# A fused attention and two-MLP kernel: another step table for the attention work inside the first MLP, and another placing of nine weight conversions

## The chip, the cores and the metric

One Trainium2 chip, one core. The metric is the device time of one execution in microseconds (us), the median of three runs. Engines are named as the profile names them: PE (TensorE matmul) and PEld (its weight loads), DVE (VectorE), ACT (ScalarE), POOL (GpSimd), SP (the engine that issues most transfers).

## What is computed

Inputs are float32. Attention has 4 batches, 8 heads, 576 rows of 64, each row looking at itself and the 63 before it. Its output is the input of a first MLP with a layer norm ahead of it, and that one's output is the input of a second block that mixes the tokens and then the channels.

```python
scores = scale * np.matmul(q, k.transpose(0, 1, 3, 2))
mask = (rel >= 0) & (rel < 64)
attn = softmax(np.where(mask, scores, -1e9))
x = (attn @ v)                                # 4 x 576 x 512
xn = (x - mu) / np.sqrt(var + 1e-06) * g_ln
x = x + np.maximum(xn @ w_ch1, 0.0) @ w_ch2   # first MLP, 512 -> 2048 -> 512
h = np.maximum(xt @ w_tok1, 0.0) @ w_tok2     # second block, over the tokens
u = x + h.transpose(0, 2, 1)
out = u + np.maximum(u @ w_ch1, 0.0) @ w_ch2  # 512 -> 1536 -> 512
```

## The kernel before

The 2304 rows are 18 tiles of 128. The first MLP runs in five blocks of tiles, `BLOCKS`: 3, 3, 4, 4 and 4 tiles; they are called blocks 0 to 4 here. Every product is made from float32 numbers split in a high and a low part, in three passes, so a product of a 128-row chunk takes three matmuls.

**A block** is `mlp_block` (L430): 16 steps f, one for each 128 columns of the hidden layer. In a step `mm1` (L400) makes the hidden chunk `ha` with 12 matmuls (L409), ACT takes its positive part (L413) and DVE the low part of that (L421, called the low part below); then `mm2` (L424) adds an earlier chunk, `LAG` = 2 steps back, into the accumulators `acca` (L427, three matmuls for each tile of the block). Between the two stand the step's hooks, functions that issue other work. `ha` has two buffers in PSUM (tag `h`), so the matmuls of `ha` of step f+2 need the low part of step f done. In block 1 the `mm2` of two steps stand together, after the odd steps. At the end of a block ACT and DVE write the next block's normalized input (L373, L374) and DVE adds the accumulators to the rows (L879).

**The hooks of blocks 1 to 3** make the attention of the next block's four tiles, by the table `STEPS` (L752): one string per step, for block 1 and for blocks 2 and 3. In it

- S is the scores of a tile: 32 small matmuls (L207), 8 maxima with the mask on DVE (L220) and 8 exponentials on ACT (L228), and then the loads of the next tile's q and k; `S4` belongs to the next block's first tile
- T*n is n of the 16 transposes of 32x256 on DVE that turn a tile's probabilities (L275)
- V is their product with v (32 matmuls into `o`, L312), the division by the sums on DVE (L318) and the load of the next v. From tile 10 on (blocks 2 and 3) `o` is one of the two buffers of `ha`
- L is the row statistics and the centring on ACT (L336 to L338), with two small POOL operations
- X*n is n of the 16 transposes of the centred rows of two tiles on DVE (L390)

A digit after S, T, V, L is the tile in its block of four, after X the pair. What stands in a step's string is issued in that order behind the step's low part, and each engine runs its instructions in the order of issue.

**The pieces.** Nine blocks of later weights come in 64 bits per number and are turned into a high and a low float32 part, in the same blocks. The table `EARLY` (L732) gives a place in `xs` and steps g = 16 (block - 1) + f: at g - 2 SP issues the load (L622), at g ACT shrinks (L130) and DVE narrows (L139, L140), at g + 1 ACT and POOL split (L122, L123), at g + 2 SP issues the store to DRAM (L641). `piece_raw`, `piece_narrow` and `piece_split` (L616 to L636) name the buffers: two rows of `xs` and a third for the narrowed words.

**Block 4** has no attention: its hooks convert the second block's first weights (b_narrow L720, w1_mix L677, w1_plain L685, w1_mixed L692, w1_keep L697), two per two steps, with scratch from the list `narrows` (L101).

**The second block** ends in `quad` (L1000), seven products per call into two PSUM buffers; ACT copies the first one to the scratch `s1` (L1013), which the last low part of the call before still reads.

```python
 752          STEPS = ((),
 753                   ("V0 S1 L0", "T1*6", "T1*8", "T1*2", "V1 S2 L1", "T2*6", "T2*8", "T2*2 X0*6", "V2 S3 L2", "X0*5 T3*3",
 754                    "T3*8", "T3*5 X0*5", "V3 L3 S4", "X1*8", "X1*8"),
 755                   ("T0*10", "T0*6", "V0 S1 L0", "T1*6", "T1*10", "V1 S2 L1", "T2*6", "T2*6", "T2*4 X0*4", "V2 S3 L2",
 756                    "X0*6 T3*3", "T3*8", "T3*5 X0*6", "V3 L3 S4", "X1*6", "X1*10"))
```

Of the kernel before, what the change touches and what calls it, by code (L numbers as in the profile page):

```python
# [12 lines left out]
U32 = mybir.dt.uint32  # L13
# [5 lines left out]
B, H, S, D = 4, 8, 576, 64  # L19
# [5 lines left out]
T1 = 256  # L25
# [49 lines left out]
def mixer_kernel(ctx, tc, qT, kT, v, g, wa1, wa2, tok1, tok2, wb1, wb2, out):  # L75
# [44 lines left out]
    def split(dst_hi, dst_lo, src, lo_engine):  # L120

        nc.scalar.activation(out=dst_hi, in_=src, func=AF.Copy)  # L122
        lo_engine.tensor_tensor(out=dst_lo, in0=src, in1=dst_hi.bitcast(F32), op=ALU.subtract)  # L123
# [134 lines left out]

    whole, wholeT, sums = {}, {}, {}

    def tile_S(t):

        whole[t] = by_heads(wide_a)
        sums[t] = stp.tile([P, 2, NH, 1], F32, tag="sums", name=f"sums{t}")
        att_S(t, False)
        for u in (2 * t, 2 * t + 1):
            att_E(u)

    def tile_T_part(t, n):
# [58 lines left out]
    def ln_scalar(t):  # L328

        m_ = mv[t] = mvp.tile([P, 2], F32, tag="mv", name=f"mv{t}")  # L330
        if t < BLOCKS[2][0]:
            x_, y_ = xh[t], _ = next_s(), next_s()
        else:
            j = (t - BLOCKS[2][0]) % 4
            x_, y_ = (lns[:, 2], lns[:, 3], reg[:, 1], reg[:, 9])[j], reg[:, 8]
        nc.scalar.activation(out=x_, in_=xt[t], func=AF.Copy, scale=-1.0 / DM, accum_out=m_[:, 0:1])  # L336
        nc.scalar.activation(out=x_, in_=xt[t], func=AF.Identity, bias=m_[:, 0:1])
        nc.scalar.activation(out=y_, in_=x_, func=AF.Square, accum_out=m_[:, 1:2])  # L338
        nc.gpsimd.tensor_scalar(out=m_[:, 1:2], in0=m_[:, 1:2], scalar1=1.0 / DM, scalar2=LN_EPS,  # L339
                                op0=ALU.mult, op1=ALU.add)  # L340
        nc.gpsimd.tensor_tensor(out=m_[:, 1:2], in0=m_[:, 1:2], in1=mhalf, op=ALU.pow)
# [109 lines left out]
    with tc.manual_schedule():  # L451
# [162 lines left out]
        early = {}  # L614

        def piece_raw(x):  # L616
            return xs[:, x:x + 2].rearrange("p t n -> p (t n)")

        def piece_load(x, piece):
            early[x] = piece  # L620
# [8 lines left out]

        def piece_narrow(x):  # L630
            n = piece_width(x)
            narrow([(xs[:, x + 2, 0:n].bitcast(U32), piece_raw(x)[:, 0:2 * n].bitcast(U32))])

        def piece_split(x):
            n, pair = piece_width(x), piece_raw(x).rearrange("p (a n) -> p a n", a=2).bitcast(F32R)
            split(pair[:, 0, 0:n], pair[:, 1, 0:n], xs[:, x + 2, 0:n], nc.gpsimd)  # L636

        def piece_keep(x):
            pair = piece_raw(x).rearrange("p (a n) -> p a n", a=2)
# [89 lines left out]

        EARLY = {12: (12, 17, 21), 15: (14, 18, 22, 26, 30, 34)}  # L732
        pieces = [t1_piece(0), t1_piece(1), t2_piece(0), t2_piece(1), rest_piece()]
        pieces += [w2_piece(q, k) for q in range(2) for k in range(2)]
        starts = sorted((g_, x) for x, gs in EARLY.items() for g_ in gs)
# [6 lines left out]
        def early_hooks(g_, hooks):  # L742
            for d, fn, x, piece in sorted(at[g_], key=lambda e: -e[0]):
# [4 lines left out]
                else:  # L748
# [1 line left out]


        STEPS = ((),  # L752
# [4 lines left out]
        done = collections.Counter()  # L757


        for i in range(NBLOCKS):  # L760
            hooks = {f: [] for f in range(FA + 2)}
            if i < NBLOCKS - 1:
                u0 = 2 * TPB * (i + 1)
                lean = i == 0

                def next_qk(t):
                    if t + 1 < NT:
                        place_fixed(t + 1)
                        load_qk(t + 1)

                def next_v(t):
                    if t + 1 < NT:
                        load_v(t + 1)

                for k in range(2 * TPB if lean else 0):
                    def s1(u=u0 + k):
                        new_x(u // 2)
                        att_S(u // 2, True)
                        next_qk(u // 2)

                    def s3(u=u0 + k):
                        att_PV(u // 2, (u % 2,))
                        if u % 2 == 1:
                            next_v(u // 2)
                            ln_stats(u // 2)

                    u, t = u0 + k, (u0 + k) // 2
                    fs, ft, fv = LEAN[k]
                    if k % 2 == 0:
                        hooks[fs].append(s1)  # L790
                    hooks[ft].insert(0, lambda u=u: att_T(u))
                    hooks[fv].append(s3)
                    if k % 2 == 1:
                        hooks[fv + 1].append(lambda t=t: ln_center(t))

                def step(op, t, n):
                    if op == "S":
                        new_x(t)
                        tile_S(t)
                        next_qk(t)  # L800
                    elif op == "V":
                        tile_PV(t)
                        next_v(t)
                    elif op == "L":
                        ln_scalar(t)
                    else:
                        (tile_T_part if op == "T" else xh_part)(t, n)

                for f, ops in enumerate(STEPS[min(i, 2)]):
                    for op in ops.split():  # L810
                        what, _, n = op.partition("*")
                        a = what[0], int(what[1]) + (0 if what[0] == "X" else BLOCKS[i + 1][0])
                        for _ in range(int(n or 1) if a[1] < NT else 0):
                            hooks[f].append(lambda a=(*a, done[a] % 16): step(*a))
                            done[a] += 1

                if lean:
                    hooks[FA - 2].append(lambda: step("S", 2 * TPB, 0))
                if i == NBLOCKS - 2:
                    hooks[FA - 1].append(lambda: b_load(2))  # L820
                for f in range(FA):
                    early_hooks(FA * (i - 1) + f, hooks[f])

                def tr3(i=i):
                    for c in range(3):
                        trans("a", xh, i + 1, c)
                if lean:
                    hooks[FA - 1].append(tr3)
                    for hh in range(2):
                        hooks[FA + hh].append(lambda hh=hh: tile_T_PE(2 * TPB, hh))  # L830

                def after(i=i):
                    if i > 0:
                        u_ = lns.rearrange("p j (c n) -> p c j n", c=KD)
                        for c in range(KD):
                            gained(xn4[:, c], c, u_[:, c], j=4)
                    else:
                        for c in range(3):
                            evac(c)
                        trans("a", xh, i + 1, 3)  # L840
                        evac(3)
            else:
                def ysk(k):
                    new_ys(0, k)
                    for t in range(2 * k, min(2 * k + 2, 9)):
                        y_split(t, nc.gpsimd)
                for f in range(1, 2 * HALF + 1):
                    hooks[f - 0.5] = [b_narrow]
                    hooks[f].append(b_shrink)
                for k, q in enumerate(ORDER):  # L850
                    hooks[2 * k + 2].append(lambda q=q: w1_mix(q))
                    hooks.setdefault(2 * k + 2.5, []).insert(0, lambda q=q, k=k: w1_plain(q, MIX_SLOT[k]))
                    hooks.setdefault(2 * k + 3.5, []).append(lambda q=q: w1_mixed(q))
                    if k < 4:
                        hooks[2 * k + 5].append(lambda q=q: w1_keep(q))
                for f, k in ((11, 0), (12, 1), (13, 2), (14, 3), (15, 4)):
                    hooks[f].append(lambda k=k: ysk(k))
                hooks[13].append(load_t1)
                hooks[14].append(lambda: load_t2(0))
                hooks[15].append(lambda: load_t2(1))  # L860

                def after():
                    pass
            if i == 0:
                later_s += [narrows.pop(), narrows.pop()]
                for f in range(FA):
# [4 lines left out]
                hooks[FA - 2].append(lambda: wnarrow(2))  # L871
            if i == 1:
                narrows[:] = [reg[:, 1]] + [lns[:, k] for k in range(4)]
            base, nt = BLOCKS[i]
            x_, m = places(nt * P), 4 if i == 1 else 3
            acc = mlp_block(i, W, FA, [(xn4 if nt > TPB else xnt)[:, c] for c in range(KD)], hooks, after, i == 1, (x_[0:m], x_[m:2 * m]))
# [120 lines left out]
        def low(role, src):  # L997
            low_h(hx[role], src)

        def quad(n, acc, jobs):  # L1000

# [52 lines left out]
        for p in range(PAIRS):  # L1054
            old = acc
            for q in range(HALF):
# [64 lines left out]
                for m, k, js in ((0, 8, (3, 4)), (0, 9, (5, 0)), (1, 0, (1, 2))):  # L1121
                    if q == m and p > 0:
                        jobs[k] += [lambda j=j, p=p, old=old: store(2 * TPB * (p - 1) + j, old[j]) for j in js]
                quad(n, old if q == 0 else acc, jobs)


        last, half = 2 * TPB * (PAIRS - 1), DM // 2
# [51 lines left out]
```

## Time and profile before

| | us |
|---|---|
| three runs, median | 820.92 (819.51 to 821.58) |
| the profiled execution | 820.49 |
| its span in the trace | 818.7 |
| DVE busy | 500.3 (61%) |
| ACT busy | 324.5 (40%) |
| POOL busy | 175.8 (21%) |

The span is the time from the first to the last recorded instruction; 1.79 us of the profiled execution lie outside it. In the trace block 1 begins at 107.17 us, block 2 at 186.80, block 3 at about 291, block 4 at about 393. A row of the timeline merges instructions of one kind that follow each other: start, length, engine, line, operation, what is written from what, their number, and in brackets the idle time of the engine ahead of it with what ended it. Lengths of merged rows hold the last instruction's latency, so rows can overlap by some tenths. PEclk is the granted clock of TensorE as a share of 2.4 GHz.

### The profile page before, as it was taken

How to read it: one execution, taken by the hardware profiler on the slowest of the kernel's cores; microseconds unless marked ns; L12 is line 12 of the kernel's file. 1: busy time of each engine (PE TensorE's matmuls, PEld its weight loads, DVE VectorE, ACT ScalarE, POOL GpSimd, SP SyncE). 2: the span in 40 equal slices, each digit the busy share in tenths (PEclk: the TensorE clock that was granted, in tenths of full speed). 3: DMA queues.
4: the chain of work that ended last, by engine and by line, in shares of the span. 5: the costliest groups of instructions: out<-in, count | busy, mean ns of one | idle time of the engine just before them, and what ended most of it. 6: DMA issues, size and time to landing. Idle time of an engine off the chain costs nothing.

```text
span 818.7 us, 12590 instructions
## 1 busy us (share of the span) xinstructions
PE 798.7 (98%) x4730; PEld 686.8 (84%) x4730; DVE 500.3 (61%) x1162; ACT 324.5 (40%) x802; POOL 175.8 (21%) x181
## 2 busy tenths in 40 slices
PE   8999989998999989999999999999999999999998
PEld 6788878886888868888888888888988998998997
DVE  5898757788666786566855326756565644742223
ACT  6887643343434324331443422423453222432221
POOL 3655400010110000000033724311134000310000
PEclk9999999998999999999999999999999999999999
DMA  9798321242432222110258315234551624235302
GB/s 338 239 293 280 100 66 52 84 136 79 146 105 86 87 67 79 51 52 27 71 176 317 147 42 208 88 142 152 179 195 79 257 91 175 94 105 219 114 1 77
DMA packets 34284, 108.42 MB, mean 132 GB/s; under 512 B 4912, under 2 KB 6448, under 8 KB 31024
## 3 DMA queue, kind: packets, MB, share of 16 engines
q1 hardware_dynamic: 34080, 107.36, 38.0%
q8 instruction: 37, 0.61, 0.3%
q10 hardware_dynamic: 144, 0.26, 0.1%
q14 instruction: 23, 0.19, 0.1%
HBM read 86.77 MB, written 20.32 MB: 131 GB/s over the span
## 4 chain that ended last, share of the span: by engine, by line
PE 82%; DVE 11%; ACT 5%; issue 1%; POOL 0%; DVEq 0%; ACTq 0%
PE acca L427 19%; PE ha L409 17%; PE accb L984 17%; PE prod L975 16%; DVE reg L275 4%; PE td L911 3%; PE th L897 3%; PE o L312 2%; DVE reg L390 2%; PE s L207 2%; ACT reg L228 2%; DVE hreg L421 1%; PE accb L1135 1%; DVE xnt L374 1%; PE pt L243 1%
## 5 line engine op out<-in xcount | busy, mean ns | idle before, releaser
L409 PE MATMUL ha<-xnt,wa 128*128 128x512 f32 (+1 forms) x960 | 211.2, 370 | 3.1 <-DVE hreg L421 2.3
L427 PE MATMUL acca<-wa,hreg 128*128 128x512 f32 x864 | 211.6, 395 | 0.3 <-DVE hreg L421 0.3
L409 PEld LDWEIGHTS ha<-xnt,wa 128*128 128x128 f32 x960 | 175.2, 188 | 30.2 <-DVE hreg L421 2.6
L427 PEld LDWEIGHTS acca<-wa,hreg 128*128 128x128 f32 x864 | 161.4, 189 | 35.8 <-issue 2.0
L984 PE MATMUL accb<-w,hreg 128*128 128x512 f32 x612 | 142.2, 390 | 0.0
L984 PEld LDWEIGHTS accb<-w,hreg 128*128 128x128 f32 x612 | 114.6, 188 | 23.2
L421 DVE SCALAR_TENSOR_TENSOR hreg<-ha,hreg 128x512 fp32r<-128x512 f32 (+1 forms) x80 | 50.8, 635 | 108.6 <-ACT hreg L413 108.2
L413 ACT ACTIVATE hreg<-ha 128x512 fp32r<-128x512 f32 (+1 forms) x80 | 44.1, 552 | 172.9 <-PE ha L409 167.8
L275 DVE STREAM_TRANSPOSE reg<-reg 32x256 f32<-32x256 f32 x176 | 76.7, 436 | 2.6
L992 POOL TENSOR_TENSOR reg<-reg 128x384 f32<-128x384 f32 x18 | 18.5, 1026 | 211.4 <-ACT reg L989 211.4
L421 DVE SCALAR_TENSOR_TENSOR hreg<-reg,hreg 128x384 fp32r<-128x384 f32 x54 | 33.0, 612 | 45.9 <-ACT hreg L995 45.8
L975 PE MATMUL prod<-xm,w1b 128*128 128x384 f32 x324 | 59.6, 335 | 0.7 <-ACT reg L989 0.6
L989 ACT ACTIVATE reg<-prod 128x384 f32<-128x384 f32 x72 | 35.3, 492 | 62.9 <-PE prod L975 60.3
L228 ACT ACTIVATE reg<-reg,mx 128x128 f32<-128x128 f32 x120 | 46.5, 389 | 29.0 <-DVE mx L220 29.0
L975 PEld LDWEIGHTS prod<-xm,w1b 128*128 128x128 f32 x324 | 56.3, 188 | 1.7 <-ACT reg L989 1.4
L995 ACT ACTIVATE hreg<-reg 128x384 fp32r<-128x384 f32 x54 | 28.1, 525 | 71.7 <-PE accb L984 71.7
L992 DVE TENSOR_TENSOR reg<-prod,reg 128x384 f32<-128x384 f32 x36 | 20.0, 556 | 57.8 <-PE prod L975 56.7
L339 POOL TENSOR_SCALAR mv<-mv 128x1 f32<-128x1 f32 x13 | 2.9, 222 | 222.7 <-ACT reg L338 222.6
L390 DVE STREAM_TRANSPOSE reg<-reg 32x256 f32<-32x256 f32 x96 | 41.7, 434 | 1.5
L975 PE MATMUL prod<-xm,w1a 128*128 128x384 f32 x216 | 41.2, 337 | 0.0
L975 PEld LDWEIGHTS prod<-xm,w1a 128*128 128x128 f32 x216 | 37.8, 188 | 0.6 <-POOL xm L123 0.3
L382 DVE STREAM_TRANSPOSE reg<-xs 32x384 f32<-32x384 f32 x64 | 36.4, 569 | 1.4
(152 smaller groups left out, 953.7 us busy)
## 6 DMA issues: line engine op xcount, KB each, us to landing
xs<-in_wa SPq DMA_DIRECT2D x32, 512.0 KB, 4.8
w1b<-kept SPq DMA_DIRECT2D x16, 1024.0 KB, 7.3
w1a<-kept SPq DMA_DIRECT2D x16, 768.0 KB, 4.7
reg<-in_v SPq DMA_DIRECT2D x28, 256.0 KB, 3.2
reg<-in_wb SPq DMA_DIRECT2D x12, 512.0 KB, 4.1
kept<-w1b SPq DMA_DIRECT2D x6, 1024.0 KB, 7.8
kept<-w1a SPq DMA_DIRECT2D x6, 768.0 KB, 5.7
more<-in_wb SPq DMA_DIRECT2D x8, 512.0 KB, 3.6
```

The source lines that it names most:

```text
L228: nc.scalar.activation(out=f_[:, h], in_=f_[:, h], func=AF.Exp, scale=-1.0, bias=mx[:, h], accum_out=sm[:, h])
L275: nc.vector.transpose(out=s_[32 * b:32 * b + 32, :, 32 * a:32 * a + 32], in_=f_[32 * a:32 * a + 32, :, 32 * b:32 * b + 32])
L382: nc.vector.transpose(out=d_[:, :, :, 32 * a:32 * a + 32], in_=s_[:, :, :, 32 * b:32 * b + 32])
L390: nc.vector.transpose(out=d_[:, :, :, 32 * a:32 * a + 32], in_=s_[:, :, :, 32 * b:32 * b + 32])
L409: nc.tensor.matmul(h_, lhsT=w[:, a, c * P:(c + 1) * P], rhs=src[c][:, b], start=n == 0, stop=n == 3 * KD - 1)
L413: nc.scalar.activation(out=t_[0], in_=h_, func=AF.Relu)
L421: nc.vector.scalar_tensor_tensor(out=t_[1], in0=src, scalar=0.0, in1=t_[0].bitcast(F32), op0=ALU.max, op1=ALU.subtract)
L427: nc.tensor.matmul(acc[j], lhsT=t_[a][:, j * P:(j + 1) * P], rhs=ws[f][:, 2 + b], start=f == first and n == 0, stop=f == last and n == 2)
L975: nc.tensor.matmul(dst, lhsT=w_[:, a, c * P:(c + 1) * P], rhs=xm[m][:, c, b], start=first and n == 0, stop=n == 5, skip_group_check=True)
L984: nc.tensor.matmul(acc[j], lhsT=hx[role][a][:, (j % TPB) * P:(j % TPB + 1) * P], rhs=w2[q][:, k, b], start=q == 0 and role in ("21", "12") ...
L989: nc.scalar.activation(out=dst, in_=src, func=AF.Copy)
L992: eng.tensor_tensor(out=dst, in0=x, in1=y, op=ALU.add)
```

## The change

In blocks 2 and 3, V moves from steps 2, 5, 9, 13 to 3, 6, 10, 13; the first tile's transposes are spread 6, 6, 4 over three steps; L stands one step behind its V; 12 of a tile's 16 transposes stand in the step after its S; X1 ends at step 14. In block 1, V is at 0, 5, 9, 13, the first step's eight exponentials are issued in two halves (H1, E1), and steps 4 and 12 hold no attention. The nine pieces move: two at g = 4, two at 12, then 21, 24, 28, and 53 and 58, in block 4, in other buffers; none is left in block 3. The scratch of L's squares becomes `lns[:, j]`, where it was `reg[:, 8]`, the first half of the T buffer. In block 4 `narrows` has four buffers, not five. The second `quad` call takes another buffer for `s1`.

```diff
-    def tile_S(t):
+    def tile_S(t, half=False):
...
-        for u in (2 * t, 2 * t + 1):
+        for u in (2 * t, 2 * t + 1)[:1 if half else 2]:
             att_E(u)
...
-            x_, y_ = (lns[:, 2], lns[:, 3], reg[:, 1], reg[:, 9])[j], reg[:, 8]
+            x_, y_ = (lns[:, 2], lns[:, 3], reg[:, 1], reg[:, 9])[j], lns[:, j]
...
-            return xs[:, x:x + 2].rearrange("p t n -> p (t n)")
+            return (xs[:, x:x + 2] if x < NT else reg[:, 0:2]).rearrange("p t n -> p (t n)")
+
+        def piece_tmp(x, n):
+            return (xs[:, x + 2] if x < NT else wide_a[:, 1])[:, 0:n]
...
-        EARLY = {12: (12, 17, 21), 15: (14, 18, 22, 26, 30, 34)}
+        EARLY = {12: (4, 12, 21), 15: (4, 12, 24, 28), NT: (53, 58)}
...
-                 ("V0 S1 L0", "T1*6", "T1*8", "T1*2", "V1 S2 L1", "T2*6", "T2*8", "T2*2 X0*6", "V2 S3 L2", "X0*5 T3*3",
-                  "T3*8", "T3*5 X0*5", "V3 L3 S4", "X1*8", "X1*8"),
-                 ("T0*10", "T0*6", "V0 S1 L0", "T1*6", "T1*10", "V1 S2 L1", "T2*6", "T2*6", "T2*4 X0*4", "V2 S3 L2",
-                  "X0*6 T3*3", "T3*8", "T3*5 X0*6", "V3 L3 S4", "X1*6", "X1*10"))
+                 ("V0 H1", "E1", "T1*8", "L0 T1*8", "", "V1 S2", "L1 T2*10", "T2*6", "X0*8", "V2 S3 X0*8", "L2 T3*10",
+                  "T3*6", "", "V3 L3 S4 X1*10", "X1*6"),
+                 ("T0*6", "T0*6", "T0*4", "V0 S1", "L0 T1*12", "T1*4", "V1 S2", "L1 T2*12", "T2*4 X0*6", "X0*10", "V2 S3",
+                  "L2 T3*12", "T3*4", "V3 L3 S4 X1*8", "X1*8"))
...
+            if i == NBLOCKS - 1:
+                del narrows[0]
...
-                quad(n, old if q == 0 else acc, jobs)
+                quad(n, old if q == 0 else acc, jobs, tt[1][:, 0] if n == 1 else s1)
```

ACT at the start of block 1, from the positive part of step 0 (`ha_0`) on; the two rows of L228 are the exponentials of S1's two halves. Before:

```order
L413 ACTIVATE hreg<-ha_0_1386 128x384
L228 ACTIVATE reg,sums_1421<-reg,mx_1440 128x128 x4
L228 ACTIVATE reg,sums_1421<-reg,mx_1445 128x128 x4
L336 ACTIVATE reg,mv_1462<-xs 128x512
L337 ACTIVATE reg<-xs,mv_1462 128x512
L338 ACTIVATE reg,mv_1462<-reg 128x512
L413 ACTIVATE hreg<-ha_1_1468 128x384
```

and with the change:

```order
L413 ACTIVATE hreg<-ha_0_1386 128x384
L228 ACTIVATE reg,sums_1421<-reg,mx_1440 128x128 x4
L413 ACTIVATE hreg<-ha_1_1458 128x384
L228 ACTIVATE reg,sums_1421<-reg,mx_1445 128x128 x4
L413 ACTIVATE hreg<-ha_2_1477 128x384
L413 ACTIVATE hreg<-ha_3_1504 128x384
L336 ACTIVATE reg,mv_1519<-xs 128x512
```

The positive part of step 1 had eight exponentials and L0 ahead of it; four exponentials are left there.

PE at the start of block 2, from `ha` of step 0 to the first V (`o`). Before:

```order
L409 MATMUL ha_0_2150<-xnt,wa_430 128x512 x12
L409 MATMUL ha_1_2177<-xnt,wa_449 128x512 x12
L409 MATMUL ha_2_2203<-xnt,wa_483 128x512 x12
L312 MATMUL o_0_2219<-reg 64x64 x16
L207 MATMUL s_2240<-reg 64x128 x2
```

and with the change:

```order
L409 MATMUL ha_0_2164<-xnt,wa_430 128x512 x12
L409 MATMUL ha_1_2185<-xnt,wa_449 128x512 x12
L409 MATMUL ha_2_2206<-xnt,wa_483 128x512 x12
L427 MATMUL acca_0_2160<-wa_430,hreg 128x512 x3
L427 MATMUL acca_1_2161<-wa_430,hreg 128x512 x3
L427 MATMUL acca_2_2162<-wa_430,hreg 128x512 x3
L427 MATMUL acca_3_2163<-wa_430,hreg 128x512 x3
L409 MATMUL ha_3_2239<-xnt,wa_512 128x512 x12
L312 MATMUL o_0_2254<-reg 64x64 x16
```

The first V stands behind two more groups of 12 matmuls; block 3 begins the same way.

DVE in the same place, from the low part of step 0 to the division of the first V (L318). Before:

```order
L421 SCALAR_TENSOR_TENSOR hreg<-ha_0_2150,hreg 128x512
L275 STREAM_TRANSPOSE reg<-reg 32x8x32 x10
L421 SCALAR_TENSOR_TENSOR hreg<-ha_1_2177,hreg 128x512
L275 STREAM_TRANSPOSE reg<-reg 32x8x32 x6
L252 TENSOR_SCALAR sums_1968<-sums_1968 128x8
L253 RECIPROCAL sums_1968<-sums_1968 128x8
L139 TENSOR_SCALAR xs<-xs 128x512
L140 SCALAR_TENSOR_TENSOR xs<-xs 128x512
L421 SCALAR_TENSOR_TENSOR hreg<-ha_2_2203,hreg 128x512
L318 TENSOR_TENSOR xs<-o_0_2219,sums_1968 128x512
```

and with the change:

```order
L421 SCALAR_TENSOR_TENSOR hreg<-ha_0_2164,hreg 128x512
L275 STREAM_TRANSPOSE reg<-reg 32x8x32 x6
L421 SCALAR_TENSOR_TENSOR hreg<-ha_1_2185,hreg 128x512
L275 STREAM_TRANSPOSE reg<-reg 32x8x32 x6
L421 SCALAR_TENSOR_TENSOR hreg<-ha_2_2206,hreg 128x512
L275 STREAM_TRANSPOSE reg<-reg 32x8x32 x4
L252 TENSOR_SCALAR sums_2004<-sums_2004 128x8
L253 RECIPROCAL sums_2004<-sums_2004 128x8
L421 SCALAR_TENSOR_TENSOR hreg<-ha_3_2239,hreg 128x512
L318 TENSOR_TENSOR xs<-o_0_2254,sums_2004 128x512
```

The 16 transposes stand behind three low parts, where they stood behind two, and the piece (L139, L140) is gone from there.

## Rows read from the trace of the kernel before

**Rows 1.** The page: span, and busy time with its share by engine.

```profile
span 818.7 us, 12590 instructions
PE 798.7 (98%) x4730; PEld 686.8 (84%) x4730; DVE 500.3 (61%) x1162; ACT 324.5 (40%) x802; POOL 175.8 (21%) x181
```

**Rows 2.** Waits of PE, whole span: line, released by, total us, times, longest.

```profile
PE o L312 <- DVE reg L275: 5.6, 5, 2.4
PE o L312 <- DVE hreg L421: 2.9, 2, 1.5
...
PE prod L975 <- ACT reg L989: 0.6, 1, 0.6
...
PE acca L427 <- DVE hreg L421: 0.3, 1, 0.3
```

**Rows 3.** Timeline of PE, step 3 of block 1, idle time in brackets.

```profile
118.35 2.37 PE L409 MATMUL ha<-xnt,wa 128*128 128x384 f32 x12 [2.32 <-DVE hreg L421]
```

**Rows 4.** Timeline of ACT, block 1: first exponential, and positive parts of steps 1, 2.

```profile
112.01 0.40 ACT L228 ACTIVATE reg<-reg,mx 128x128 f32<-128x128 f32 x1 [1.96 <-DVE mx L220]
...
117.24 0.85 ACT L413 ACTIVATE hreg<-ha 128x384 fp32r<-128x384 f32 x2
```

**Rows 5.** Timeline of PE, start of block 2.

```profile
186.80 8.64 PE L409 MATMUL ha<-xnt,wa 128*128 128x512 f32 x36
196.86 0.33 PE L312 MATMUL o<-reg 128*64 128x64 f32 x2 [1.43 <-DVE hreg L421]
199.59 1.97 PE L312 MATMUL o<-reg 128*64 128x64 f32 x30 [2.40 <-DVE reg L275]
201.49 1.99 PE L207 MATMUL s<-reg 64*64 64x128 f32 x32
203.41 3.96 PE L427 MATMUL acca<-wa,hreg 128*128 128x512 f32 x12
```

**Rows 6.** Timeline of DVE, start of block 2.

```profile
191.03 0.67 DVE L421 SCALAR_TENSOR_TENSOR hreg<-ha,hreg 128x512 fp32r<-128x512 f32 x1
191.62 4.46 DVE L275 STREAM_TRANSPOSE reg<-reg 32x256 f32<-32x256 f32 x10
...
196.84 2.70 DVE L275 STREAM_TRANSPOSE reg<-reg 32x256 f32<-32x256 f32 x6
...
200.38 0.69 DVE L140 SCALAR_TENSOR_TENSOR xs<-xs 128x512 uint32<-128x512 uint32 x1
```

**Rows 7.** Granted clock in three stretches (window; busy by engine; PEclk; DMA share; GB/s).

```profile
118.00:120.00 2.00, 1.65 (x9) 1.65 (x10) 1.95 (x6) 0.09 (x1) 0.24 (x1) 1.00 0.04 8
199.00:201.00 2.00, 1.41 (x26) 1.41 (x28) 1.82 (x7) 0.00 (x0) 0.00 (x0) 0.50 0.00 0
305.00:307.00 2.00, 2.00 (x33) 1.67 (x26) 0.78 (x4) 0.00 (x0) 0.00 (x0) 0.50 0.65 203
```

**Rows 8.** Timeline of PE: second V of block 2, then first V of block 3.

```profile
221.47 1.15 PE L312 MATMUL o<-reg 128*64 128x64 f32 x30 [0.25 <-DVE reg L275]
222.55 1.10 PE L207 MATMUL s<-reg 64*64 64x128 f32 x32
223.58 3.01 PE L427 MATMUL acca<-wa,hreg 128*128 128x512 f32 x12
...
303.50 1.25 PE L312 MATMUL o<-reg 128*64 128x64 f32 x30 [2.40 <-DVE reg L275]
304.68 1.98 PE L207 MATMUL s<-reg 64*64 64x128 f32 x32
306.59 3.60 PE L427 MATMUL acca<-wa,hreg 128*128 128x512 f32 x12
```

**Rows 9.** Chain that ended last, block 2: start, length, what.

```profile
226.60 2.72 PE ha L409 x12
```

**Rows 10.** Timelines: a positive part on ACT, block 2; a low part on DVE, block 4.

```profile
190.04 0.60 ACT L413 ACTIVATE hreg<-ha 128x512 fp32r<-128x512 f32 x1 [2.37 <-PE ha L409]
...
423.52 0.69 DVE L421 SCALAR_TENSOR_TENSOR hreg<-ha,hreg 128x512 fp32r<-128x512 f32 x1 [3.32 <-ACT hreg L413]
```

More of the change, by code (lines that the diff above doesn't have):

```diff
@@ L631, in piece_narrow @@
             n = piece_width(x)
-            narrow([(xs[:, x + 2, 0:n].bitcast(U32), piece_raw(x)[:, 0:2 * n].bitcast(U32))])
+            narrow([(piece_tmp(x, n).bitcast(U32), piece_raw(x)[:, 0:2 * n].bitcast(U32))])
         def piece_split(x):
             n, pair = piece_width(x), piece_raw(x).rearrange("p (a n) -> p a n", a=2).bitcast(F32R)
-            split(pair[:, 0, 0:n], pair[:, 1, 0:n], xs[:, x + 2, 0:n], nc.gpsimd)
+            split(pair[:, 0, 0:n], pair[:, 1, 0:n], piece_tmp(x, n), nc.gpsimd)
         def piece_keep(x):
@@ L796, in step @@
                 def step(op, t, n):
-                    if op == "S":
+                    if op in "SH":
                         new_x(t)
-                        tile_S(t)
+                        tile_S(t, op == "H")
                         next_qk(t)
+                    elif op == "E":
+                        att_E(2 * t + 1)
                     elif op == "V":
@@ L820, in mixer_kernel @@
                     hooks[FA - 1].append(lambda: b_load(2))
-                for f in range(FA):
-                    early_hooks(FA * (i - 1) + f, hooks[f])
                 def tr3(i=i):
@@ L863, in after @@
                     pass
+            for f in range(FA):
+                early_hooks(FA * (i - 1) + f, hooks[f])
             if i == 0:
@@ L998, in low, with quad @@
             low_h(hx[role], src)
-        def quad(n, acc, jobs):
+        def quad(n, acc, jobs, s1):
             w1a, w1b = ws1[n]
```

## The prediction

> **What bounds the kernel now.** The page first: PE is busy for 798.7 of 818.7 us [rows 1], so the kernel ends when PE has run its matmuls, and what a change of order can give is the time in which PE stands or runs slowly. The reader should then look at PE's own waits, not at those of the other engines, which are longer and cost nothing. In the whole span PE waits for DVE's transposes ahead of V five times, 5.6 us in all, for a low part ahead of V twice, 2.9 us, once for a low part ahead of `mm2`, 0.3 us, and once for ACT in the second block, 0.6 us [rows 2]. The timeline of PE adds one wait of 2.32 us in block 1 [rows 3]. These lie in the stretches that the change rewrites.
>
> The timeline then says what each wait is. At the start of block 2, PE runs `ha` of steps 0 to 2 from 186.80 on, stands 1.43 us until the low part of step 1 has freed the buffer that `o` shares with `ha`, starts two matmuls of V0, and stands 2.40 us until the last of the first tile's 16 transposes is done [rows 5]. DVE is not idle there: low part, ten transposes from 191.62, low part, six transposes from 196.84 for 2.70 us [rows 6]. It ends at 199.54, 12.74 us after the block began, and V0 is asked for after three groups of `ha`. Block 3 starts in the same way, with 2.40 us for the transposes [rows 8].
>
> Last, the granted clock. Around 200 and around 306 us it is 0.50, that is 1.2 GHz where the rest runs at 2.4 [rows 7]. PE had stood nearly 4 us just before both. After the single wait of 2.32 us in block 1 it was 1.00 [rows 7]. So the two long stops cost more than their idle time. The same three pieces of work, V, scores and one group of `acca`, take 1.97, 1.99 and 3.96 us after the stop of block 2 [rows 5] and 1.15, 1.10 and 3.01 us in the undisturbed place of that block [rows 8], a loss of 0.82 + 0.89 + 0.95 = 2.66 us. In block 3 they take 1.25, 1.98 and 3.60 [rows 8], a loss of 0.10 + 0.88 + 0.59 = 1.57. Together 4.23 us.
>
> **The change part by part.** No matmul is added or taken away, nor any transpose, maximum or exponential. The conversions are the same in number too. So the sum is one of waits.
>
> *Start of blocks 2 and 3.* V0 now stands behind one group of `mm2` and a further `ha`: five groups of 2.72 us [rows 9], 13.6 us after the block's start at least, not three. DVE has three low parts ahead of the last transpose, not two. ACT's positive part of step 0 starts 3.24 us after the block's start and takes 0.60 [rows 5, 10], so the first low part can stand at 3.84; three low parts at 0.59 from start to start and 16 transposes at 0.446 [rows 6] give 1.8 + 7.1, and the last transpose is done at 12.8. If DVE is still held by the accumulators, as now, its first low part starts at 191.03, 4.23 after the start [rows 6], and the end is 13.2. Both are ahead of 13.6, by 0.8 or 0.4 us. The conversion that stood between the transposes and the low part of step 2 is gone (L140 for 0.69 us [rows 6] and L139, shorter). The low part of step 2, whose buffer `o` needs, comes before the last four transposes. So both waits ahead of V0 go, 2.9 + 2 x 2.40 us. What is late next is the same V0: 0.4 us is little, and each tenth by which DVE is later than worked out costs a tenth, in two places.
>
> *V1 in blocks 2 and 3.* S1 and V1 stay three steps apart, but ten of the 16 transposes lay in the step before V1 and four do now. Six fewer at 0.446 put the last one 2.7 us earlier against a wait of 0.25 [rows 8]; the 12 in the step before can hold the low part between them up by some 0.6 us. I take the wait as gone. Three such waits (here, at V1 of block 3 and at V3 of block 1) make up the rest of the 5.6 us, 5.6 - 2 x 2.40 = 0.8.
>
> *V3 in blocks 2 and 3.* S3 and V3 are three steps apart, where they were four. The distance is that of S1 and V1, with the same 12 and 4, so the same cover holds: about 1.8 us. A step has two groups, 5.44 us of matmuls [rows 9]; 12 transposes and a low part are 6.0 us of DVE, the next step 4 and one, 2.4. The two steps together fit.
>
> *Block 1.* The positive part of step 1 stood on ACT behind eight exponentials from 112.01 on and behind L0, and ran at 117.24 [rows 4]; the low part after it held up `ha` of step 3 for 2.32 us [rows 3]. With four exponentials ahead of it and L0 moved to step 3, it comes 3.2 us or more earlier (of the 5.23 us between, half of the eight exponentials, about 1.6 us, stays). The 2.32 us go. The 0.3 us of `mm2` at the block's end stood behind X1's last transposes and a narrowing, which both end earlier: gone too.
>
> *The pieces.* Two together at steps 4 and 12 of block 1 put up to four DVE operations of at most 0.69 us [rows 6] in a step, 2.8 us, where no attention stands. The new risk is on ACT: the shrink waits for a load, and the positive part of the next step is queued behind it. SP has nothing to wait for ahead of these loads but the stores of earlier pieces. No row shows such a wait; I bound it below by nothing (taking pieces away from a step cannot make matmuls shorter) and above by the largest wait that one late positive part has made, 2.32 us [rows 3], twice. It is nearer to nothing, because the load is issued two steps ahead as before. In block 4, DVE stands 3.32 us in a step before its low part [rows 10]; a narrowing of 1.4 us at most fits, twice. Without that cover it would cost 1.4 each. On SP each store waits for POOL's half of the split, and loads are queued behind it: of q, k and v in blocks 1 and 2, of the second block's weights in block 4. POOL is busy for 21% [rows 1], and these loads are issued steps ahead of their use; I put nothing there. The fifth scratch buffer that block 4 loses lies behind reads of four steps before; nothing.
>
> *The second `quad`.* Its copy to `s1` waits for the last low part of the call before, and PE for the copy: 0.6 us [rows 2]. With another buffer that is gone; ACT is idle there.
>
> *The scratch of L's squares* no longer lies in the transposes' buffer; L can stand behind the first of them at no cost.
>
> **The sum**, against the span: 818.7 - 5.6 - 2.9 - 2.32 - 0.3 - 0.6 = 807.0 from waits, and 807.0 - 4.23 = 802.8 if the clock stays up. The profiled execution was 820.49, 1.79 over its span, and the median of the runs is 0.43 above it: 802.8 + 1.79 + 0.43 = **805.0 us**.
>
> The Trainium skill's page "TensorE: Matmul & The Clock Gate", in its part on the HAM clock gate, says that the half rate is the default and that activity releases it. By it the 4.23 us go with the stops; were the two half-clock stretches set by something else, the sum would be 809.2. The trace agrees with the rule as far as it goes: both stretches, 0.50, come right behind the longest stops.
>
> **The rivals.**
> *The clock does not stay up* (809.2). Short stops between groups remain, and the clock falls all the same. For it: two stretches at 0.50 exist and V0's cover is thin. Against it: a stop of 2.32 us alone left 1.00 [rows 7]. The same page's section on a second failure mode tells of short idles between groups of matmuls that make the clock swing; this trace does not show it, as the waits of 0.25 us are not followed by a longer group of `acca` [rows 8].
> *The wait moves to the later V's; slower than before.* Twelve transposes in the step after S begin as soon as the exponentials are done. If ACT ends these later than I take it (two half sets, L and a shrink share the queue), every one of nine V's (V1 to V3 in three blocks) waits. The cover is about 1.8 us each; beyond it a lateness costs nine times itself. At 1.0 us of wait each the time is 814, at 1.8 us it is that of before, 821.2, and above 2.1 us, 823.9, it is slower. For it: S3 to V3 lost a step. Against it: V1 today waits only 0.25 us with ten transposes in its last step.
> *A load is late* at the double pieces: 805.0 plus up to 2 x 2.32 = 809.6. It adds to the first case and sets its upper side.
> *Nothing is gained*, because DVE, not the order, is short of time: DVE's 61% [rows 1] speak against it.
>
> **How the numbers follow.** A measurement of this kernel tells about 0.3%, 2.5 us, from no change: 818.5 to 823.4. All waits gone and the clock up, with some tenths left: 0.70, 803.5 to 807.5. Clock down again, or a late load: 0.12, up to 810.5. Waits at the later V's: 0.18, of which 0.08 end between 810.5 and 818.5, 0.05 within 0.3% and 0.05 above. The first two hold 0.82, so the range is 803.4 to 810.5. Faster 0.90, same 0.05, slower 0.05.
>
> **What would show it.** In the changed profile: no wait of PE for L275 above 0.5 us and none for a low part above 0.5 us between the starts of blocks 1 and 4; PEclk 1.00 throughout these blocks; the first V of blocks 2 and 3 with its 32 matmuls in one row; block 2 starting some 3 us earlier; the positive part of step 1 of block 1 about 1.6 us behind the first exponential; no wait of `prod` for ACT. A wait at V3, an ACT row of L130 with idle time ahead that ended with a transfer, or a stretch of 0.50 would show the step that is wrong. Above 811 us the prediction has failed.

## The result, and the profile after

The change takes 801.12 us against 821.04 for the kernel before (medians of six runs each), a ratio of 0.9761 [0.9747, 0.9774]: faster by 19.9 us. That is the direction forecast, but 3.9 us less than the 805.0 and 2.3 us below the range's lower end of 803.4. One of the six runs of the change took 2026 us, with PE busy for 2019.4 of them at a granted clock of 1.00 and for a reason that no run shows; the ratio leaves it out, and the rows of the change come from the same kernel run again (801.11 us, ratio 0.9759 [0.9746, 0.9772]; profiled at 801.26).

The page of the change, the lines that answer to [rows 1]:

```profile
span 799.5 us, 12581 instructions
PE 791.1 (99%) x4730; PEld 682.5 (85%) x4730; DVE 499.8 (63%) x1162; ACT 324.9 (41%) x802; POOL 175.1 (22%) x181
```

The other engines did the same work in the same time; PE's busy time fell by 7.6 us and the span by 19.2. PE's waits over the whole span, which answer to [rows 2], begin with

```profile
PE idle L457 <- POOL hreg L454: 1.3, 1, 1.3
```

All seven kinds of them stand ahead of 106.7 us. Nothing of [rows 2] is left, nor the wait of [rows 3]. The timeline of PE in the changed kernel at the starts of blocks 1 and 2 (the answer to [rows 3, 5]), and at the later V's of block 2 and the first of block 3 ([rows 8]):

```profile
106.77 2.35 PE L409 MATMUL ha<-xnt,wa 128*128 128x384 f32 x12
...
111.17 6.54 PE L409 MATMUL ha<-xnt,wa 128*128 128x384 f32 x36
...
174.31 8.36 PE L427 MATMUL acca<-wa,hreg 128*128 128x512 f32 x36
182.51 8.32 PE L409 MATMUL ha<-xnt,wa 128*128 128x512 f32 x36
190.67 2.88 PE L427 MATMUL acca<-wa,hreg 128*128 128x512 f32 x12
193.39 2.88 PE L409 MATMUL ha<-xnt,wa 128*128 128x512 f32 x12
196.20 1.15 PE L312 MATMUL o<-reg 128*64 128x64 f32 x32
197.28 1.10 PE L207 MATMUL s<-reg 64*64 64x128 f32 x32
198.32 3.02 PE L427 MATMUL acca<-wa,hreg 128*128 128x512 f32 x12
...
257.64 1.15 PE L312 MATMUL o<-reg 128*64 128x64 f32 x32
...
292.63 1.15 PE L312 MATMUL o<-reg 128*64 128x64 f32 x32
```

Every V is one row of 32 matmuls with no bracket, and V, scores and `acca` take 1.15, 1.10 and 3.02 us behind the start of block 2, the undisturbed figures of [rows 8]. DVE ahead of those V's: the last four transposes of tiles 0 and 3 of block 2 and of tile 0 of block 3:

```profile
193.52 1.79 DVE L275 STREAM_TRANSPOSE reg<-reg 32x256 f32<-32x256 f32 x4
...
254.23 1.79 DVE L275 STREAM_TRANSPOSE reg<-reg 32x256 f32<-32x256 f32 x4
...
289.95 1.79 DVE L275 STREAM_TRANSPOSE reg<-reg 32x256 f32<-32x256 f32 x4
```

They end at 195.31, 256.02 and 291.74, and PE comes to the V's 0.9, 1.6 and 0.9 us later. That is the whole cover of these V's. The windows of blocks 1 to 3 (columns as in [rows 7]) say most in one number. Before:

```profile
107.00:393.00 286.00, 274.93 (x1846) 230.10 (x1845) 200.78 (x568) 103.95 (x315) 20.53 (x33) 0.98 0.25 80
```

and with the change:

```profile
107.00:374.00 267.00, 267.00 (x1840) 225.15 (x1839) 200.08 (x567) 102.11 (x311) 17.53 (x31) 1.00 0.24 78
```

PE was idle for 286.00 - 274.93 = 11.07 us there and is idle for none now, at full clock. But by the table below the three blocks together became 18 us shorter, not 11: some 7 us went from time that the profile calls busy. By stage, from the start of the first PE row of each:

| stage | before: start | length | change: start | length | difference | forecast |
|---|---|---|---|---|---|---|
| ahead of block 1 | 0 | 107.17 | 0 | 106.77 | -0.40 | 0 |
| block 1 | 107.17 | 79.63 | 106.77 | 75.74 | -3.89 | -2.9 |
| block 2 | 186.80 | 104.17 | 182.51 | 96.43 | -7.74 | -6.7 |
| block 3 | 290.97 | 101.80 | 278.94 | 95.38 | -6.42 | -5.7 |
| block 4 | 392.77 | 87.04 | 374.32 | 87.04 | 0 | 0 |
| token mixing | 479.81 | 47.17 | 461.36 | 47.17 | 0 | 0 |
| quads | 526.98 | 280.02 | 508.53 | 279.28 | -0.74 | -0.6 |
| the rest | 807.00 | 11.70 | 787.81 | 11.69 | 0 | 0 |

The forecast of a stage is the sum of its terms in the prediction (block 2: 1.43 + 2.40 + 0.25 + 2.66). Every stage in which a stop went gained more than its terms, and no other stage gained but the first, whose length was 106.56 to 107.17 in all the traces though nothing differs there. The blocks repeat far better than whole executions do: in every trace in which nothing waits there, block 1 took 75.74 us (four traces), block 2 96.43 (four) and block 3 95.39 (five), each to 0.01. So tenths of a block can be read. The quads spread more: 279.07 to 279.28 in the four traces without the old `s1`, 279.99 to 280.49 in the five with it.

### The profile page after: what moved, and what is told of

It is laid out like the page before. It is cut to its first block, busy times and chain, and to the rows that moved or that the text cites. A ratio compares the mean times of both kernels' runs of the same rounds, so it can differ in the third digit from the quotient of the medians.

```text
span 2024.4 us, 12581 instructions
## 1 busy us (share of the span) xinstructions
PE 2019.4 (100%) x4730; PEld 1306.0 (65%) x4730; DVE 501.6 (25%) x1162; ACT 325.7 (16%) x802; POOL 171.8 (8%) x181
## 4 chain that ended last, share of the span: by engine, by line
PE 99%; DVE 0%; issue 0%
PE acca L427 25%; PE ha L409 25%; PE accb L991 18%; PE prod L982 17%; PE td L918 4%; PE th L904 3%; PE o L312 2%; PE s L207 2%; PE accb L1142 1%; PE pt L243 1%; PE tpa L355 0%; PE tpu L355 0%; PE idle L533 0%; PE ptw L288 0%; PE prod L1142 0%; DVE xs L1052 0%
## 5 line engine op out<-in xcount | busy, mean ns | idle before, releaser
L409 PE MATMUL ha<-xnt,wa 128*128 128x512 f32 (+1 forms) x960 | 530.4, 771 | 0.0
L427 PE MATMUL acca<-wa,hreg 128*128 128x512 f32 x864 | 529.8, 828 | 0.0
L409 PEld LDWEIGHTS ha<-xnt,wa 128*128 128x128 f32 x960 | 336.0, 351 | 183.5 <-issue 179.3
L427 PEld LDWEIGHTS acca<-wa,hreg 128*128 128x128 f32 x864 | 298.8, 348 | 202.9 <-issue 197.3
L991 PE MATMUL accb<-w,hreg 128*128 128x512 f32 x612 | 368.3, 828 | 0.0
L991 PEld LDWEIGHTS accb<-w,hreg 128*128 128x128 f32 x612 | 215.3, 352 | 144.0 <-issue 143.3
L982 PE MATMUL prod<-xm,w1b 128*128 128x384 f32 x324 | 149.1, 682 | 0.0
L982 PE MATMUL prod<-xm,w1a 128*128 128x384 f32 x216 | 100.9, 681 | 0.0
L918 PE MATMUL td<-h,t 128*128 128x512 f32 x120 | 73.7, 831 | 0.0
L904 PE MATMUL th<-ys,t 128*128 128x512 f32 x112 | 68.0, 834 | 0.0
```

Of the source, the lines that this page charges most:

```text
L409: nc.tensor.matmul(h_, lhsT=w[:, a, c * P:(c + 1) * P], rhs=src[c][:, b], start=n == 0, stop=n == 3 * KD - 1)
L427: nc.tensor.matmul(acc[j], lhsT=t_[a][:, j * P:(j + 1) * P], rhs=ws[f][:, 2 + b], start=f == first and n == 0, stop=f == last and n == 2)
L904: nc.tensor.matmul(p_, lhsT=a, rhs=b_, start=n == 0, stop=n == len(ops) - 1)
L918: nc.tensor.matmul(p_, lhsT=t2[tt][:, a, col:col + P], rhs=h1[b][:, tt, c], start=n == 0, stop=n == last)
L982: nc.tensor.matmul(dst, lhsT=w_[:, a, c * P:(c + 1) * P], rhs=xm[m][:, c, b], start=first and n == 0, stop=n == 5, skip_group_check=True)
L991: nc.tensor.matmul(acc[j], lhsT=hx[role][a][:, (j % TPB) * P:(j % TPB + 1) * P], rhs=w2[q][:, k, b], start=q == 0 and role in ("21", "12") ...
```

## The experiments

The question is where the missing 2.9 us of blocks 1 to 3 and the quads come from. **R**: PE loses more at a stop than the bracket shows. The bracket begins where the last matmul ends by the profile, and that end holds its latency; without the stop the next one would have started earlier. **B**: a stop costs its bracket, and the rest lies elsewhere: in a faster pace of the undisturbed groups (**P**), in a half clock that cost more than 4.23 us (**C**), or in parts of the kernel that the sum did not name (**E**).

**The change again, and its three parts alone**, all beside one set of runs of the kernel before (820.7 us).

> The changed kernel once more, for a trace. Theory of the prediction (the gain is PE's waits, 11.7 us, and the half-clock stretches, 4.2 us): span 802.8, PE waits below 1 us between blocks 1 and 4, and the time of each block shorter by just its waits and clock. The measured 801.1 says some 4 us more went. Rival P (pace): undisturbed groups of matmuls in blocks 1 to 3 are a little faster too, so a block's time falls by more than its listed waits, in block 1 by 3.7 where the waits are 2.9. Rival C (clock): the whole loss at half clock was larger than the three pieces compared, up to half of the time at 0.50. Rival E (elsewhere): 1 us or more goes in block 4 or in the second block, from 393 us on.

It gave 801.11 us, ratio 0.9759 [0.9746, 0.9772], and the rows shown above. E falls by the table: block 4, token mixing and the rest stand still. P falls too: a group of `mm2` takes 193.39 - 190.67 = 2.72 us, and three of `ha` take 190.67 - 182.51 = 8.16, 2.72 each as in [rows 9].

The table of blocks 2 and 3 alone, with the squares' scratch that it needs there:

```diff
+                 ("T0*6", "T0*6", "T0*4", "V0 S1", "L0 T1*12", "T1*4", "V1 S2", "L1 T2*12", "T2*4 X0*6", "X0*10", "V2 S3",
+                  "L2 T3*12", "T3*4", "V3 L3 S4 X1*8", "X1*8"))
...
-..., reg[:, 8]
+..., lns[:, j] if t >= BLOCKS[3][0] else reg[:, 8]
```

> Kernel before with the new table for blocks 2 and 3 alone (and the squares' scratch there). Theory of the prediction: the waits ahead of V0 and V1 of blocks 2 and 3 (2.9 + 4.8 + 0.5) and the clock (4.2) go, 12.4 us: 808.6, less by up to 1 because two pieces still stand on DVE at the start of block 2. Rival C: 811 falls to 807 or lower, the clock's share being above 4.2. Rival P: below 807 too, but with the starts of the blocks alone explaining 12.4.

807.93 us, ratio 0.9842 [0.9829, 0.9856]: 12.8 us of the gain. Its timeline of PE in block 2, to the start of block 3:

```profile
186.59 8.67 PE L409 MATMUL ha<-xnt,wa 128*128 128x512 f32 x36
...
200.62 0.33 PE L312 MATMUL o<-reg 128*64 128x64 f32 x2
201.25 1.15 PE L312 MATMUL o<-reg 128*64 128x64 f32 x30 [0.30 <-DVE reg L275]
...
283.98 8.32 PE L409 MATMUL ha<-xnt,wa 128*128 128x512 f32 x36
```

Block 2 takes 97.39 us, 0.96 more than in the change. A piece still stands on DVE ahead of the last transposes there, and V0 waits for them. So with the new order the removal of the piece is worth a wait whose bracket is 0.30. From the start of the first two matmuls to that of the others it is 0.63, and all of that is lost: the 30 behind a wait take 222.55 - 221.47 = 1.08 us [rows 8], as long as the 32 without one (197.28 - 196.20). The other 0.35 lies inside the first row, 8.67 long where the change has 8.32: the first group of `ha` waits there for DVE's normalized input, and no bracket shows it.

The table of block 1 alone, with the halves of the exponentials:

```diff
+                 ("V0 H1", "E1", "T1*8", "L0 T1*8", "", "V1 S2", "L1 T2*10", "T2*6", "X0*8", "V2 S3 X0*8", "L2 T3*10",
+                  "T3*6", "", "V3 L3 S4 X1*10", "X1*6"),
...
+..., lns[:, j] if t < BLOCKS[3][0] else reg[:, 8]
```

> Kernel before with the new table for block 1 alone (halved exponentials, squares' scratch there). Theory of the prediction: 2.32 + 0.3 us of waits go: 818.2, with the 0.3 at the block's end kept if the piece at its step 14 makes it. Rival P: 817.3 or lower, block 1 shorter by 3.5 or more.

815.05 us, ratio 0.9929 [0.9916, 0.9941]. PE at the starts of blocks 1, 2 and 4:

```profile
107.14 2.35 PE L409 MATMUL ha<-xnt,wa 128*128 128x384 f32 x12
...
182.87 8.32 PE L409 MATMUL ha<-xnt,wa 128*128 128x512 f32 x36
...
386.92 8.32 PE L409 MATMUL ha<-xnt,wa 128*128 128x512 f32 x36
```

Block 1 is as long as in the change, 75.73 us, 3.90 shorter than before, for terms of 2.9. The run was expected at 818.2; 815.05 and a block shorter by more than 3.5 are what its expectation set as the sign of P. They don't show P, as the groups are no faster: 18 matmuls of `acca` in block 1 take 4.12 us in both kernels and 24 of `ha` 4.18 or 4.19. Only their order does something: a V and its scores between a group of `ha` and one of `acca` cost 0.04 us less than between two of `ha`, three times in the block. Blocks 2 and 3, whose table is the old one, take 204.05 us where they took 205.97.

The pieces alone, with their buffers and the four buffers of `narrows` (the old tables of steps, the old `s1`):

```diff
-        EARLY = {12: (12, 17, 21), 15: (14, 18, 22, 26, 30, 34)}
+        EARLY = {12: (4, 12, 21), 15: (4, 12, 24, 28), NT: (53, 58)}
...
+            if i == NBLOCKS - 1:
+                del narrows[0]
```

> Kernel before with the pieces moved alone (two in block 4), the tables of steps as before. Theory of the prediction: the pieces as such cost nothing; away from the end of block 1 and the starts of blocks 2 and 3 they free DVE by 1.1 us there, worth up to 1.1 us at the start of block 2; at steps 4 and 12 they now meet V, S and L and may cost as much. 818 to 822. Rival E: 817 or lower, with the gain in block 4 or later.

818.64 us, ratio 0.9972 [0.9960, 0.9984]: 2.1 us. PE at the starts of blocks 1 and 2:

```profile
107.13 2.36 PE L409 MATMUL ha<-xnt,wa 128*128 128x384 f32 x12
...
186.20 8.32 PE L409 MATMUL ha<-xnt,wa 128*128 128x512 f32 x36
195.66 0.33 PE L312 MATMUL o<-reg 128*64 128x64 f32 x2 [1.14 <-DVE hreg L421]
198.39 1.77 PE L312 MATMUL o<-reg 128*64 128x64 f32 x30 [2.40 <-DVE reg L275]
200.09 1.99 PE L207 MATMUL s<-reg 64*64 64x128 f32 x32
202.01 3.04 PE L427 MATMUL acca<-wa,hreg 128*128 128x512 f32 x12
```

Block 1 takes 79.07 us, 0.56 less than before; the wait that went at its end had a bracket of 0.26. In block 2 the wait of 2.40 stands as it did, so the piece that stood behind the transposes there was not what V0 waited for. The half-clock stretch behind it cost 0.62 + 0.89 + 0.03 = 1.54 us by the undisturbed figures of [rows 8], where before it cost 2.66 for nearly the same stops.

The three parts give 12.8 + 5.65 + 2.06 = 20.5 us, and with the `s1` of 0.8 (below) 21.3, where the change gives 19.6. They overlap in block 1's last wait, which two of them remove, and the second and third profit from a shorter half-clock stretch that the first removes whole.

**Single stops put back into the change**, beside 820.37 us for the kernel before. Each tells R from B: by B the stage grows by the bracket that comes back, by R by some 0.2 to 0.3 more.

Block 1 with L0 and the whole S1 in step 1 again:

```diff
-                 ("V0 H1", "E1", "T1*8", "L0 T1*8", "", ...
+                 ("V0 S1 L0", "", "T1*8", "T1*8", "", ...
```

> The change, but the first step of block 1 as before: all eight exponentials and L0 there. Block 1 runs 75.7 us in the change. Both theories: one stop of PE, bracketed 2.3 us, comes back at the matmuls of step 3. Theory R (a stop costs more than its bracket, because the bracket begins only at the modelled end of the last matmul): block 1 gets 2.6 us longer. Theory B (brackets are the cost): 2.3 us, 78.0. The whole kernel 803.4 to 803.8.

803.74 us, ratio 0.9802 [0.9786, 0.9819], 2.6 above the change. PE, from block 1 to the start of block 2:

```profile
106.56 2.35 PE L409 MATMUL ha<-xnt,wa 128*128 128x384 f32 x12
110.97 4.46 PE L409 MATMUL ha<-xnt,wa 128*128 128x384 f32 x24
117.74 2.35 PE L409 MATMUL ha<-xnt,wa 128*128 128x384 f32 x12 [2.32 <-DVE hreg L421]
...
184.90 8.32 PE L409 MATMUL ha<-xnt,wa 128*128 128x512 f32 x36
```

The bracket is 2.32 as in [rows 3], and block 1 takes 78.34 us, 2.60 more than in the change. This is R in one stop. Its place shows why: the next group starts 117.74 - 110.97 = 6.77 us after the 24 matmuls did, and 24 such matmuls with no wait behind them take 139.52 - 135.34 = 4.18 in the kernel before (the other rows here are for the table further down):

```profile
111.57 4.46 PE L409 MATMUL ha<-xnt,wa 128*128 128x384 f32 x24
...
135.34 4.35 PE L409 MATMUL ha<-xnt,wa 128*128 128x384 f32 x24
139.52 4.28 PE L427 MATMUL acca<-wa,hreg 128*128 128x512 f32 x18
...
178.03 6.78 PE L427 MATMUL acca<-wa,hreg 128*128 128x512 f32 x29
...
220.90 0.33 PE L312 MATMUL o<-reg 128*64 128x64 f32 x2
...
300.77 0.33 PE L312 MATMUL o<-reg 128*64 128x64 f32 x2 [1.49 <-DVE hreg L421]
```

So 2.59 were lost. The row of the 24 is 4.46 long, 0.28 more than the 4.18 for which they keep the next group waiting, and the bracket counts from its end. The clock has no part in it, 1.00 behind this stop:

```profile
117.00:119.00 2.00, 1.26 (x7) 1.26 (x8) 1.84 (x5) 0.48 (x2) 0.55 (x1) 1.00 0.84 309
```

The whole S1 in step 1, with L0 left at step 4:

```diff
-                 ("V0 H1", "E1", "T1*8", "L0 T1*8", "", ...
+                 ("V0 S1", "", "T1*8", "L0 T1*8", "", ...
```

> The change, but the exponentials of block 1's first step whole again, L0 left where the change puts it. If L0's move carries the gain, the low part of step 1 ends about 0.5 us after it is wanted: a stop of 0 to 0.6 us in the trace. If the halving carries it, a stop of 1.5 us or more. Whole kernel 801 to 802, or 802.6 and more.

801.73 us, ratio 0.9775 [0.9761, 0.9790]. PE, from block 1 to the start of block 2:

```profile
106.75 2.36 PE L409 MATMUL ha<-xnt,wa 128*128 128x384 f32 x12
...
115.80 2.35 PE L409 MATMUL ha<-xnt,wa 128*128 128x384 f32 x12 [0.19 <-DVE hreg L421]
...
182.95 8.32 PE L409 MATMUL ha<-xnt,wa 128*128 128x512 f32 x36
```

Block 1 takes 76.20, 0.46 more than in the change, for a bracket of 0.19. It also splits the two edits: of the 2.60 us, moving L0 gave 2.1 and halving the exponentials 0.46.

The old scratch `s1` for all `quad` calls:

```diff
-                quad(n, old if q == 0 else acc, jobs, tt[1][:, 0] if n == 1 else s1)
+                quad(n, old if q == 0 else acc, jobs, s1)
```

> The change, but the second quad with the old scratch. One stop bracketed 0.6 us comes back. Theory R: from the first quad to the last group of accumulators 0.7 to 0.9 us more (279.3 to 280.1), theory B: 0.6. Whole kernel 801.7 to 802.

801.90 us, ratio 0.9778 [0.9763, 0.9793]. PE at the start of the quads, at the wait that came back, and at the start of the rest:

```profile
508.77 1.23 PE L982 MATMUL prod<-xnt,w1a 128*128 128x384 f32 x6
...
525.88 3.42 PE L982 MATMUL prod<-xm,w1b 128*128 128x384 f32 x18 [0.59 <-ACT reg L996]
...
788.76 7.68 PE L1142 MATMUL accb<-w,hreg 128*128 128x512 f32 x36
```

The stage takes 279.99 us, 0.71 more than in the change, for a bracket of 0.59. Beside the other traces without this stop it is 0.8 to 0.9 more, so R holds here by 0.1 us at least, with a spread of 0.2 between traces.

V0 and S1 at step 2 again in blocks 2 and 3, with the first tile's transposes 10 and 6, nothing else:

```diff
-                 ("T0*6", "T0*6", "T0*4", "V0 S1", "L0 T1*12", "T1*4", ...
+                 ("T0*10", "T0*6", "V0 S1", "", "L0 T1*12", "T1*4", ...
```

> The change, but in blocks 2 and 3 the first tile's transposes 10, 6 and V0 and S1 at step 2, as before. The two stops of PE ahead of V0 come back in both blocks, some 1.0 and 2.4 us by their brackets, and the half clock with them. Theory B plus the clock as taken in the prediction (1.6 to 2.7 us per block): 5.0 to 6.1 us per block. Theory R: 0.5 us more for the two stops. If the clock does not fall, 3.4 to 3.9 per block. Whole kernel: 811 to 814; 808 to 809 without the clock.

811.97 us, ratio 0.9902 [0.9884, 0.9920]: 10.9 us, more than half of the gain, hang on this one step in two blocks. PE in block 2 and at the starts of blocks 3 and 4:

```profile
182.33 8.32 PE L409 MATMUL ha<-xnt,wa 128*128 128x512 f32 x36
191.73 0.33 PE L312 MATMUL o<-reg 128*64 128x64 f32 x2 [1.07 <-DVE hreg L421]
194.46 1.97 PE L312 MATMUL o<-reg 128*64 128x64 f32 x30 [2.40 <-DVE reg L275]
196.36 1.60 PE L207 MATMUL s<-reg 64*64 64x128 f32 x32
197.88 3.02 PE L427 MATMUL acca<-wa,hreg 128*128 128x512 f32 x12
200.73 2.88 PE L409 MATMUL ha<-xnt,wa 128*128 128x512 f32 x12
...
283.93 8.32 PE L409 MATMUL ha<-xnt,wa 128*128 128x512 f32 x36
...
384.69 8.32 PE L409 MATMUL ha<-xnt,wa 128*128 128x512 f32 x36
```

and its granted clock behind the stops:

```profile
195.00:197.00 2.00, 2.00 (x38) 1.88 (x38) 0.93 (x2) 0.00 (x0) 0.00 (x0) 0.50 0.00 0
```

Blocks 2 and 3 take 101.60 and 100.76 us, 5.17 and 5.38 more than in the change. From start to start the first stop is 191.73 - 182.33 = 9.40 against 8.25 for three groups of `ha` with a V behind them (two of 2.72 and one of 196.20 - 193.39 = 2.81), a loss of 1.15; the second is 194.46 - 191.73 = 2.73, all of it lost: together 3.88 where the brackets are 3.47. The rest is the half clock: the three pieces of work take 200.73 - 194.46 = 6.27 us, where they take 4.97 at full clock behind the short stop at V1 of block 2 in the kernel before: 1.30. 3.88 + 1.30 = 5.18, for 5.17 measured. In block 3 the same reading gives 1.50. The clock is down, 0.50, behind the stops that were put back and stays at 1.00 where they are gone. The Trainium skill's page "TensorE: Matmul & The Clock Gate", Part 1, holds that the half rate is the default and activity lifts it; these traces agree. C falls: by the same reading the half clock cost 207.21 - 199.59 - 4.97 = 2.65 and 310.03 - 303.50 - 4.97 = 1.56 us in the kernel before, for the 4.23 of the sum, and the group of `ha` behind each stretch takes its 2.72 us again.

## Why the prediction was right and wrong

**Right: the mechanisms and their places.** All ten waits of the sum went, with the two half-clock stretches, and nothing took their place. DVE's last transpose for V0 of block 2 ended 12.80 us after the block's start, forecast at 12.8 or 13.2; V0 started 13.69 after it, forecast at 13.6; the cover is 0.9 us, where 0.8 and 0.4 were worked out. The cover of V3 is 1.6 where 1.8 was worked out, so the rival of waits at the later V's did not come. In block 1 the positive part of step 1 started 1.97 us after the first exponential, forecast 1.6; ACT was free after 1.65, and the 0.32 in the bracket are a wait for PE:

```profile
111.61 0.40 ACT L228 ACTIVATE reg<-reg,mx 128x128 f32<-128x128 f32 x1 [1.96 <-DVE mx L220]
...
113.58 0.49 ACT L413 ACTIVATE hreg<-ha 128x384 fp32r<-128x384 f32 x1 [0.32 <-PE ha L409]
```

None of the nine pieces' loads kept a shrink on ACT waiting. In block 4 two loads of the second block's weights did, for 0.40 and 0.85 us, where the kernel before had one such wait, 0.85, and PE waited for neither; block 4, where narrowings went, kept its 87.04 us, so the late loads and the narrowings cost nothing. The rival that the clock falls all the same is wrong too: 1.00 throughout blocks 1 to 3 of this trace.

**Wrong: the size of each stop.** The step that failed is the sum's first line, 818.7 - 5.6 - 2.9 - 2.32 - 0.3 - 0.6, in which each stop was entered with its idle time. Put back one by one, stops with brackets of 2.32, 0.19 and 0.59 lengthened their stages by 2.60, 0.46 and 0.71. The same reading, from start to start, of the kernel before:

| stop before | rows | from start to start, less the work | bracket |
|---|---|---|---|
| block 1, `ha` of step 3 | 3 | 118.35 - 111.57 - 4.18 = 2.60 | 2.32 |
| block 1, end, `acca` | - | 186.80 - 178.03 - 8.20 = 0.57 | 0.26 |
| block 2, `o`, first stop | 5 | 196.86 - 186.80 - 8.25 = 1.81 | 1.43 |
| block 2, `o`, second stop | 5 | 199.59 - 196.86 = 2.73 | 2.40 |
| block 2, V1 | 8 | 221.47 - 220.90 = 0.57 | 0.25 |
| block 3, first stop | 8 | 300.77 - 290.97 - 8.25 = 1.55 | 1.49 |
| block 3, second stop | 8 | 303.50 - 300.77 = 2.73 | 2.40 |

The 4.18, 8.25 and 8.20 are such work without a wait: 24 matmuls as shown for block 1, three groups of `ha` with a V behind them, and the 36 last matmuls of block 1 in the change (182.51 - 174.31). At the second stops and at V1 the 30 matmuls behind the wait take as long as a whole V without one, so nothing is taken off. Two losses stand in no bracket at all: 0.32 us inside the first row of block 2 (8.64 long, in the change 8.32), where the first group of `ha` waited for DVE's normalized input, and some 0.14 at the end of block 1, where that group itself started late. The waits at V1 of block 3 and at V3 of block 1 were short by 0.32 each like V1 of block 2, and the one in the quads by 0.14. So the ten stops explain 2.8 of the 2.9 us; the last 0.1 is the order of the V's in block 1. With each stop at its size the forecast would have been 802.2, also below the range.

**What else parts 805.0 from 801.1.** The change's trace was 0.40 us quicker ahead of block 1, where no instruction differs: that is luck. And 0.43 us was added because the median of before lay so much above its profiled execution; the change's lies 0.15 below its own. The 0.43 should not have been carried over whole, since the executions of the kernel before differ by their half clock (last section), which the change does not have. So 805.0 - 2.9 - 0.4 - 0.6 = 801.1. The range failed for the same reason as the sum: its lower end allowed for left-over waits and for none that cost more than they showed.

## What to carry to other kernels

Size a stop of a pipelined engine from the start of the work ahead of it to the start of the work behind it, less the time that the same work takes where nothing waits; the idle time in brackets was a lower bound at every stop here, short by 0.06 to 0.38 us and mostly by 0.3. Take the undisturbed time from the same work in the same order: a group of `ha` takes 2.72 us ahead of `mm2` and 2.81 ahead of a V. Where one stop follows another closely, read the granted clock behind them as well, because the slow stretch there is counted as busy. A consumer moved one step later pays when its input is done within that step: here two V's moved behind two more groups of matmuls gave 10.9 of 19.9 us.

## What was not expected of the hardware

The half clock behind nearly equal stops was not equally dear: the same three pieces of work lost 2.66 us in block 2 of the kernel before, 1.54 there with the pieces alone, 1.30 and 1.50 in the two blocks with V0 put back. That need not come from the programs, as it differs between executions of one program too: 17 of the kernel before took 821.0 to 821.9 us at a mean granted clock of 0.992, 820.1 to 820.6 at 0.994 and 818.1 at 0.996. What sets the moment at which the full clock returns was not tried.

A single stop may now and then cost the clock as well. With the 2.6 us stop put back in block 1 the trace shows 1.00 behind it, and three executions took 803.4 to 803.9 us at 1.000; the fourth took 804.86 at 0.998. The table of blocks 2 and 3 alone, which keeps this stop, gives 807.26 and 807.36 at 1.000 and 808.50 and 808.55 at 0.998 and 0.997. The change without it stayed at 0.999 or more in all ten executions. Where in the executions below 0.999 the clock fell is not recorded, so it is not shown that the stop was the cause.

And the wait with a bracket of 0.19 us alone cost 0.46: what a bracket leaves out does not grow with it, 0.27 us here and 0.28 for the one of 2.32.
